# Linear attention into a two-layer MLP on one core: the third batch's x transposed by DMA instead of TensorE, with loads and k preparation of three batches placed elsewhere

## The chip, the core and the metric

The kernel runs on one core of a Trainium2 chip. TensorE (PE) multiplies matrices; VectorE (DVE), ScalarE (ACT) and GpSimd (POOL) do elementwise work; SyncE (SP) issues nearly all DMAs. Each engine runs its own instructions in program order and waits for others by semaphores. The metric is device time in microseconds: the median of three runs before is 295.06 us (294.76 to 298.65).

## The reference

Cosine-weighted linear attention over 8 batches, 8 heads, 576 positions and head width 64, and then a two-layer MLP with a leaky ReLU over the 4608 rows that come out.

```python
def phi(x, c, s):
    r = np.maximum(x, 0.0)
    return np.concatenate([r * c, r * s], axis=-1)   # cos and sin of the position
q_p, k_p = phi(q, cos_w, sin_w), phi(k, cos_w, sin_w)
kv  = np.einsum('bhsf,bhsd->bhfd', k_p, v)
z   = np.sum(k_p, axis=2)
num = np.einsum('bhsf,bhfd->bhsd', q_p, kv)
den = np.einsum('bhsf,bhf->bhs', q_p, z)[..., None] + 1e-06
x = (num / den).transpose(0, 2, 1, 3).reshape(4608, 512)
h = x @ w_in                                         # 512 -> 2048
out = np.maximum(0.01 * h, h) @ w_out                # 2048 -> 512
```

## The kernel before

**Tiles.** Of each batch's 576 positions, 512 are the main part, in four tiles of 128 rows (j = 0 to 3). The 64 left over of all eight batches make a ninth group of 512 rows. So the MLP goes over nine groups g, numbered from 0; the third batch is number 2. All matmuls are in fp16.

**Attention of a batch b.** q, k and v come in as one load of 1 MB each (`load_main`, L86), k and v each with two loads of 64 KB for the left-over rows (`load_kvtail`, L96). `q_prep`, `k_main` and `k_tail` apply phi (L226 on VectorE, L224 on ScalarE). `v_main` and `v_tail` cast v (L232 on ScalarE), with a column of ones for the denominator. `q_transpose_dma` (L334) transposes each q tile by DMA. `kv_all` does 8 matmuls on the left-over rows (L290) and 32 on the main part (L299), and ScalarE copies the result out (L306). `num` does 8 matmuls per tile j (L363), and VectorE divides (L374, L378, L379) and writes x as xs. `num` uses a PSUM pool of one buffer, so the next `num` waits for this divide; `kv_all` uses the same pool.

**x transposed.** The MLP needs x with its 512 columns on the partitions, as xT. For the batches from 3 on this is a DMA transpose per tile (`x_transpose_dma`, L345). For batch 2 it is four TensorE transposes per tile (`x_transpose`, L429) into PSUM and a ScalarE copy (L430). Batches 0 and 1 use TensorE in another form, which the change leaves as it is.

**The MLP.** `f1(g, m)` is four matmuls of 512 columns (L443) for one of 16 column tiles m; after each second one, ScalarE applies the leaky ReLU to the pair (L451). `f2(g, i)` is four matmuls (L466) into an output tile (four calls per tile of 128 rows); after the fourth, VectorE copies the tile out (L234) and SyncE stores it (L480).

**What sets the order.** Past the first two batches the program's order is written by hand. `units` holds f1 and f2 with a position each: 16 positions for each g, in which f2 of g alternates with f1 of g + 1. The table `ahead` says how many f2 calls come before the first f1 of the next batch. All attention work is put in as steps `at(position, function)`, and `weave` emits each step before the first unit whose position is not below its own. A position thus sets the order on every engine and DMA queue; when an instruction really runs depends on its waits. Helpers put whole series at once:

- `load_steps(b, pk, pv, pq)`: k with its two tails at pk, v with its two at pv, q at pq.
- `q_steps(b, start, step, lag)`: q preparation of tile j at start + j step, its DMA transpose lag later.
- `kv_steps(b, start, step, mm, eng_v)`: k tail at start, k pieces every step, v casts on an engine, `kv_all` at mm. The casts begin at start + 3 step, 0.1 apart, for b up to 3, and at start + 1.5 step, 1 apart, for b above 3.
- `out_steps(b, start, step, lag)`: `num` of tile j at start + j step, the DMA transpose of its x lag later.

Each DMA issue on SyncE also waits for the DMA eight before it to land.

Of the kernel before, what the change touches and what calls it, by code (L numbers as in the profile page):

```python
# [9 lines left out]
dt = mybir.dt  # L10
# [3 lines left out]
P = 128  # L14
J = 4
# [3 lines left out]
def kernel(  # L19
# [14 lines left out]
    nc = tc.nc  # L34
# [8 lines left out]
    NKC = DM // P  # L43
# [28 lines left out]
    def psum(where, shape, dtype, name):  # L72
        p = {"h": ps_h, "o": ps_o, "n": ps_n}[where]
        return p.tile(shape, dtype, name=name, tag="ps_" + where)

    st = {}
    ACT, DVE, POOL = nc.scalar, nc.vector, nc.gpsimd
# [85 lines left out]
    def idle(n):  # L163
# [10 lines left out]
    ident = const.tile([P, P], dt.float16, name="ident")  # L174
# [10 lines left out]
        base=0,  # L185
# [3 lines left out]
    for o in range(2):  # L189
# [3 lines left out]
            base=MAIN,  # L193
# [145 lines left out]
    def xT_tile(g, j):  # L339
        if ("xT", g) not in st:  # L340
            st["xT", g] = xtpool.tile([P, NKC, MAIN], dt.float16, name="xT")
        return st["xT", g][:, :, j * P : (j + 1) * P]
# [79 lines left out]
                st["xT", g][:, 2 * hg : 2 * hg + 2, jp * 2 * P : (jp + 1) * 2 * P], ps  # L422
            )

    def x_transpose(g, j, where="o"):
        xs = st["xs", g, j]
        ps = psum(where, [P, NKC, P], dt.float16, "ps_xt")
        for c in range(NKC):
            nc.tensor.transpose(ps[:, c, :], xs[:, 2 * c : 2 * c + 2, :], ident)  # L429
        nc.scalar.copy(xT_tile(g, j), ps)  # L430

    def ffn1(g, m, lo=0, hi=MAIN, chunks=range(NKC), where="h"):
# [117 lines left out]
    ps = psum("h", [P, 2, 512], dt.float32, "ps_numh")  # L552
# [44 lines left out]
    def f1(g, m, where="h"):  # L597
        return lambda: ffn1(g, m, where=where)

    def f2(g, i):  # L600
        return lambda: ffn2(g, i)
# [3 lines left out]
    def at(pos, f, *args):  # L605
        steps.append((pos, lambda: f(*args)))
# [22 lines left out]
    ps = psum("n", [P, 2, DM], dt.float32, "ps_o")  # L629
# [24 lines left out]
    ps = psum("h", [P, 2, MAIN], dt.float16, "ps_x")  # L654
# [22 lines left out]
    for m in range(6, NFT):  # L677
        units.append((8 + m / 2, f1(1, m)))
    for g in range(1, NG):
        ahead = {1: 8, 2: 4}.get(g, 0)  # L680
        order = [f2(g, i) for i in range(ahead)]
        for i in range(16):
            if g + 1 < NG:
                order.append(f1(g + 1, i))
            if ahead + i < 16:
                order.append(f2(g, ahead + i))
        for n, u in enumerate(order):
            units.append((16 * g + 16 * n / len(order), u))
# [3 lines left out]
    def kv_steps(b, start, step, mm, eng_v, n_act=0):  # L692
        at(start - 0.01, kp_tiles, b)
        at(start, k_tail, b, DVE, DVE)
        for i in range(J):
            at(start + (i + 1) * step, k_main, b, i, ACT if i < n_act else DVE, DVE)
        v0, dv = (start + 1.5 * step, 1) if b > 3 else (start + 3 * step, 0.1)
        at(v0, v_main, b, 0, 4, eng_v)
        at(v0 + dv, v_main, b, 4, 8, eng_v)
        at(v0 + 2 * dv, v_tail, b, eng_v)  # L700
        at(mm, kv_all, b)

    def load_steps(b, pk, pv, pq):
        at(pk, load_k, b)
        at(pv, load_v, b)
        at(pq, load_main, "q", q, b)

    def out_steps(b, start, step, lag):
        for j in range(J):
            at(start + j * step, num, b, j)  # L710
            at(start + j * step + lag, x_transpose_dma, b, j)

    def q_steps(b, start, step, lag):
        for j in range(J):
            at(start + j * step, q_prep, b, j)
            at(start + j * step + lag, q_transpose_dma, b, j)

    q_steps(2, 8, 0.4, 0.3)
    kv_steps(2, 9.7, 0.5, 14, DVE, 2)
    for j in range(J):  # L720
        at(14.5 + 1.1 * j, num, 2, j)
        at(15.8 + 1.1 * j, x_transpose, 2, j, "o" if j < 2 else "h")

    load_steps(3, 11, 13, 10)
    q_steps(3, 18, 0.8, 0.8)
    kv_steps(3, 20, 0.7, 24, ACT)
    out_steps(3, 24.5, 1.4, 1)

    load_steps(4, 21.4, 22.5, 21.3)
    kv_steps(4, 28, 1.2, 34, ACT)  # L730
    q_steps(4, 30, 0.8, 0.8)
    out_steps(4, 36.8, 2, 1.6)

    for b in range(5, NG):
        base = 16 * (b - 2)
        if b < B:
            load_steps(b, base - 14.5, base - 13, base - 14.6)
            kv_steps(b, base - 9.5, 1.4, base - 2, ACT)
        else:
            for j in range(J):  # L740
                at(base - 11.5 + 2 * j, load_qtail, j)
        q_steps(b, base - 8, 2, 1)
        out_steps(b, base + 1, 2, 1.6)
# [32 lines left out]
```

## Time and profile before

| what | value |
|---|---|
| median of three runs | 295.06 us |
| the profiled execution | 295.4 us, span 293.6 us, granted TensorE clock 0.999 |
| f1 matmuls, L443 | 592, 142.8 us busy |
| f2 matmuls, L466 | 560, 139.5 us busy |
| x transposes of batch 2, L429 | 16, and 4 ScalarE copies (L430) of 0.58 us |
| DMA transposes: q (L334), x (L345) | 28 and 24, median 3.3 and 3.7 us from issue to landing |
| k, v and q loads of 1 MB | median 9.8, 9.0 and 6.9 us to landing |
| DMA moved | 56.93 MB, mean 194 GB/s |

A row of a timeline or chain is the start in us from the beginning of the span, the length in us, then engine, line, operation and count. Where a wait stands in brackets, it is the idle time before the row and what ended it. In a timeline a matmul group's length includes its way through the array, so groups overlap; in the chain of waits each piece is cut where the next begins, and four matmuls of 512 columns take 0.86 us. The profiled execution's time is its span and 1.8 us around it.

### The profile page before, as it was taken

The page shows a single profiled execution, that of the slowest core. Times are in us where ns is not written, and L with a number is a line of the kernel's source. Part 1 is how long each engine was busy: PE and PEld are TensorE (multiplying, and loading weights), DVE is VectorE, ACT ScalarE, POOL GpSimd, SP SyncE. Part 2 cuts the span into 40 slices and gives each one's busy share as a digit, 9 for nine tenths or more (in the row PEclk, how much of TensorE's full clock was granted, in tenths as well). Part 3 has the DMA queues.
Part 4 walks back from the last instruction along what each step waited for, and adds up shares of the span by engine and source line. Part 5 has one row for each costly group of instructions (what it writes and reads, how often), then busy time and mean ns, then how long its engine had stood idle before and what let it go on. Part 6 is the DMA issues. An engine that isn't in the chain of part 4 may idle for free.

```text
span 293.6 us, 4865 instructions
## 1 busy us (share of the span) xinstructions
PE 286.6 (98%) x1958; PEld 152.6 (52%) x1958; DVE 128.7 (44%) x328; ACT 118.3 (40%) x148; POOL 12.6 (4%) x24
## 2 busy tenths in 40 slices
PE   8899999999999998999999999999999999999995
PEld 3585466555555554555545554555444444444444
DVE  6841687936836714923562346233333311000011
ACT  6856266753544631642453226322222232222200
POOL 2264000000000000000000000000000000000000
PEclk9999999999999999999999999999999999999999
DMA  7999999999999999989664998716671211011133
GB/s 230 346 387 407 321 362 335 313 193 334 200 285 320 180 258 343 163 173 332 170 148 84 279 259 180 111 54 143 136 169 56 71 54 38 36 45 59 42 70 73
DMA packets 88933, 56.93 MB, mean 194 GB/s; under 512 B 56912, under 2 KB 81744, under 8 KB 88528
## 3 DMA queue, kind: packets, MB, share of 16 engines
q1 hardware_dynamic: 88832, 56.57, 74.3%
q8 instruction: 15, 0.25, 0.4%
q10 hardware_dynamic: 80, 0.07, 0.1%
q14 instruction: 6, 0.05, 0.0%
HBM read 36.70 MB, written 9.44 MB: 157 GB/s over the span
## 4 chain that ended last, share of the span: by engine, by line
PE 88%; DMA 6%; SPq 3%; DVE 1%; ACT 1%; issue 0%; DVEq 0%
PE ps_h L443 40%; PE ps_o L466 39%; DMA ktl<-in_k_dram 3%; PE ps_num L363 2%; PE ps_kv L299 2%; DMA vst<-in_v_dram 2%; SPq L96 1%; SPq L86 1%; DMA out_dram<-osb 1%; PE ps_xth L417 1%; PE ps_qt L353 1%; PE ps_numh L399 1%; PE ps_kv L290 0%; PE ps_idle L166 0%; PE ps_kvh L274 0%
## 5 line engine op out<-in xcount | busy, mean ns | idle before, releaser
L443 PE MATMUL ps_h<-xT,w 128*128 128x512 f16 (+1 forms) x592 | 142.8, 373 | 0.1
L466 PE MATMUL ps_o<-w,g 128*128 128x512 f16 x560 | 139.5, 379 | 0.0
L451 ACT ACTIVATE g<-ps_h 128x1024 f16<-128x1024 f32 x72 | 73.2, 1023 | 125.2 <-PE ps_h L443 125.2
L443 PEld LDWEIGHTS <-w 128*128 128x128 f16 x592 | 64.4, 114 | 52.3 <-issue 0.2
L466 PEld LDWEIGHTS <-g 128*128 128x128 f16 x560 | 54.2, 98 | 61.4
L234 DVE COPY osb<-ps_o 128x512 f32<-128x512 f32 x31 | 21.4, 691 | 79.3 <-PE ps_o L466 78.5
L374 DVE TENSOR_SCALAR den<-ps_num 128x8 f32<-128x8 f32 x28 | 4.6, 165 | 51.0 <-PE ps_num L363 51.0
L379 DVE TENSOR_TENSOR xs<-ps_num,rden 128x512 f16<-128x512 f32 x28 | 19.4, 691 | 1.0
L226 DVE TENSOR_SCALAR kpm<-kst,sin_t 128x512 f16<-128x512 f32 (+1 forms) x40 | 16.6, 430 | 1.3 <-DMA kst<-in_k_dram 1.3
L226 DVE TENSOR_SCALAR qp<-qst,cos_t 128x512 f16<-128x512 f32 (+1 forms) x34 | 15.5, 456 | 2.7 <-DMA qst<-in_q_dram 2.7
L226 DVE TENSOR_SCALAR qp<-qst,sin_t 128x512 f16<-128x512 f32 (+1 forms) x34 | 15.5, 456 | 0.0
L232 ACT CAST vmain<-vst 128x1024 f16<-128x1024 f32 (+1 forms) x14 | 12.8, 919 | 6.0 <-DMA vst<-in_v_dram 5.9
L363 PEld LDWEIGHTS <-qpT 128*128 128x128 f16 (+1 forms) x256 | 10.6, 101 | 8.4 <-issue 3.1
L226 DVE TENSOR_SCALAR kpm<-kst,cos_t 128x512 f16<-128x512 f32 (+1 forms) x29 | 13.2, 454 | 0.4 <-DMA kst<-in_k_dram 0.3
L363 PE MATMUL ps_num<-kv,qpT 128*128 128x66 f16 (+1 forms) x256 | 11.8, 194 | 0.9 <-DVE xs L379 0.9
L166 PE MATMUL ps_idle<-blank 128*128 128x512 f16 x30 | 10.0, 483 | 1.2 <-DVE blank L161 1.2
L234 DVE CAST w<-w2st 128x1024 f16<-128x1024 f32 (+1 forms) x6 | 5.1, 868 | 11.5 <-DMA w2st<-in_moe_w_out_dram 11.4
L232 ACT COPY qpT<-ps_qt 128x1024 f16<-128x1024 f16 x7 | 7.0, 1012 | 6.0 <-PE ps_qt L353 6.0
L234 POOL CAST w<-w1st 128x1024 f16<-128x1024 f32 (+1 forms) x9 | 8.5, 946 | 3.4 <-DMA w1st<-in_moe_w_in_dram 3.3
L378 DVE RECIPROCAL rden<-den 128x8 f32<-128x8 f32 x36 | 7.3, 203 | 1.2
L299 PE MATMUL ps_kv<-vmain,kpm 128*128 128x66 f16 x192 | 7.2, 194 | 0.0
L306 ACT CAST kv<-ps_kv 128x528 f16<-128x528 f32 x6 | 3.6, 599 | 7.5 <-PE ps_kv L299 7.5
(62 smaller groups left out, 102.6 us busy)
## 6 DMA issues: line engine op xcount, KB each, us to landing
out_dram<-osb SPq DMA_DIRECT2D x32, 256.0 KB, 2.9
qst<-in_q_dram SPq DMA_DIRECT2D x7, 1024.0 KB, 6.9
kst<-in_k_dram SPq DMA_DIRECT2D x6, 1024.0 KB, 9.8
vst<-in_v_dram SPq DMA_DIRECT2D x6, 1024.0 KB, 9.0
w1st<-in_moe_w_in_dram SPq DMA_DIRECT2D x7, 512.0 KB, 10.3
w2st<-in_moe_w_out_dram SPq DMA_DIRECT2D x3, 1024.0 KB, 12.9
kst<-in_k_dram SPq DMA_DIRECT2D x4, 512.0 KB, 7.2
vst<-in_v_dram SPq DMA_DIRECT2D x4, 512.0 KB, 8.1
```

The costliest lines, as they stand in the source:

```text
L166: nc.tensor.matmul(ps, lhsT=blank[:, 0:P], rhs=blank)
L226: eng.tensor_scalar(out=o, in0=i, scalar1=0.0, scalar2=col, op0=ALU.max, op1=ALU.mult)
L232: nc.scalar.copy(o, i)
L234: eng.tensor_copy(o, i)
L299: nc.tensor.matmul(ps[:, h % 2, h // 2], lhsT=kpm[:, h, j, :], rhs=vmain[b % 2][:, h, j, :], start=False, stop=(h >= H - 2 and j == J - 1),)
L363: nc.tensor.matmul(ps[lo:hi, h // 4, (h % 4) * NE : (h % 4 + 1) * NE], lhsT=qpT[:, h, lo:hi], rhs=kv[b][:, h, :],)
L374: nc.vector.tensor_scalar_add(den.rearrange("p (a b) -> p a b", a=2), ps[:, :, D : 4 * NE : NE], 1e-6)
L378: nc.vector.reciprocal(rden, den)
L379: nc.vector.tensor_tensor(out=xs, in0=ps[:, :, 0 : 4 * NE].rearrange("p a (b e) -> p a b e", e=NE)[:, :, :, 0:D], in1=rden.rearrange("p (a ...
L443: nc.tensor.matmul(ps[:, m % 2, lo:hi], lhsT=w1[m // 4, c][0][:, w1[m // 4, c][1], m % 4 : 512 : 4], rhs=xT[:, c, lo:hi], start=(c == 0 an ...
L451: nc.scalar.activation(st["g", g][:, m - 1 : m + 1, :], ps, AF.Lrelu)
L466: nc.tensor.matmul(st["ps_o", g, tt], lhsT=st["g", g][:, m, tt * P : (tt + 1) * P], rhs=w2[:, m, :], start=(m == 0), stop=(m == NFT - 1),)
```

## The change

- Batch 2's x is transposed by four DMA transposes instead of sixteen TensorE transposes and four ScalarE copies; its `num` steps stand 0.9 apart instead of 1.1 and begin at 14.4 instead of 14.5. `x_transpose` goes.
- Twelve f2 calls of batch 1, instead of eight, stand ahead of the first f1 of batch 2.
- Batch 3's k and v loads move from 11 and 13 to 16.2 and 18, so that on SyncE they come between the x transposes of batch 2: two of these, k and its tails, one, an output, one, v and its tails. Its q load stays at 10. Its q, k, v preparation, `kv_all` and x move back by 0.5 to 1.
- Batch 4's loads move from 21.3 to 22.5 to 24 to 25.1, its preparation and `kv_all` (34 to 36.5) back by 1.5 to 2.5.
- Batch 5's loads come 2 positions later. For batches 5, 6 and 7, the k preparation starts 2 positions later with steps of 1.2 instead of 1.4, and `kv_all` 0.5 later.

Between the second f1 of batch 2 and `kv_all` of batch 3 there are now f2, f1, f2; before there were f2, f1, f2, f1, f2. The v casts of batch 3 stand on ScalarE directly behind the leaky ReLU of that second f1, as before.

```diff
@@ -421,13 +421,6 @@
             nc.scalar.copy(
                 st["xT", g][:, 2 * hg : 2 * hg + 2, jp * 2 * P : (jp + 1) * 2 * P], ps
             )
-
-    def x_transpose(g, j, where="o"):
-        xs = st["xs", g, j]
-        ps = psum(where, [P, NKC, P], dt.float16, "ps_xt")
-        for c in range(NKC):
-            nc.tensor.transpose(ps[:, c, :], xs[:, 2 * c : 2 * c + 2, :], ident)
-        nc.scalar.copy(xT_tile(g, j), ps)
 
 
 
@@ -677,7 +670,7 @@
     for m in range(6, NFT):
         units.append((8 + m / 2, f1(1, m)))
     for g in range(1, NG):
-        ahead = {1: 8, 2: 4}.get(g, 0)
+        ahead = {1: 12, 2: 4}.get(g, 0)
         order = [f2(g, i) for i in range(ahead)]
         for i in range(16):
             if g + 1 < NG:
@@ -717,25 +710,24 @@
 
     q_steps(2, 8, 0.4, 0.3)
     kv_steps(2, 9.7, 0.5, 14, DVE, 2)
-    for j in range(J):
-        at(14.5 + 1.1 * j, num, 2, j)
-        at(15.8 + 1.1 * j, x_transpose, 2, j, "o" if j < 2 else "h")
-
-    load_steps(3, 11, 13, 10)
-    q_steps(3, 18, 0.8, 0.8)
-    kv_steps(3, 20, 0.7, 24, ACT)
-    out_steps(3, 24.5, 1.4, 1)
-
-    load_steps(4, 21.4, 22.5, 21.3)
-    kv_steps(4, 28, 1.2, 34, ACT)
-    q_steps(4, 30, 0.8, 0.8)
-    out_steps(4, 36.8, 2, 1.6)
+    out_steps(2, 14.4, 0.9, 0.8)
+
+    load_steps(3, 16.2, 18, 10)
+    q_steps(3, 18.5, 0.8, 0.8)
+    kv_steps(3, 21, 0.7, 25, ACT)
+    out_steps(3, 25.5, 1.4, 1)
+
+    load_steps(4, 24.1, 25.1, 24)
+    kv_steps(4, 30, 1.2, 36.5, ACT)
+    q_steps(4, 31.5, 0.8, 0.8)
+    out_steps(4, 38, 1.8, 1.6)
 
     for b in range(5, NG):
         base = 16 * (b - 2)
         if b < B:
-            load_steps(b, base - 14.5, base - 13, base - 14.6)
-            kv_steps(b, base - 9.5, 1.4, base - 2, ACT)
+            late = 2 if b == 5 else 0
+            load_steps(b, base - 14.5 + late, base - 13 + late, base - 14.6 + late)
+            kv_steps(b, base - 7.5, 1.2, base - 1.5, ACT)
         else:
             for j in range(J):
                 at(base - 11.5 + 2 * j, load_qtail, j)
```

## The prediction

> **What bounds the kernel now.** I read the page first: shares of the span, then the chain that ended last.
>
> ```profile
> PE 286.6 (98%) x1958; PEld 152.6 (52%) x1958; DVE 128.7 (44%) x328; ACT 118.3 (40%) x148; POOL 12.6 (4%) x24
> ...
> PE 88%; DMA 6%; SPq 3%; DVE 1%; ACT 1%; issue 0%; DVEq 0%
> ```
>
> TensorE is busy 98% of 293.6 us and carries 88% of the chain; the others have slack. So I count two things: work taken off TensorE, and places where it waits. The list of waits, cut to TensorE, has only 0.9 us (for xs, L379) after the start-up. Next the chain in time around the third batch's num and x transposes, and around that wait (start, us, what).
>
> ```profile
> 66.29 0.26 PE ps_num L363 x8
> 66.54 0.22 PE ps_xt L429 x4
> 66.76 1.73 PE ps_o L466 x8
> ```
>
> ```profile
> 105.85 8.51 DMA ktl<-in_k_dram
> ...
> 114.46 0.62 DVE kpt L226 x2
> 115.08 0.09 DVE den L374
> ...
> 116.26 0.42 PE ps_num L363 x8
> 116.67 0.87 PE ps_h L443 x4
> ```
>
> Four transposes cost the chain 0.22 us, four 512-column matmuls 0.86 (call that a unit), a num 0.26. At 114 a k-tail load is late, the VectorE queue stands behind it with a divide in it, and TensorE waits for the divide. Then the ScalarE timeline before kv_all of the fourth batch, and SyncE's around two sets of loads (start, us, engine, line, operation).
>
> ```profile
> 77.54 1.02 ACT L451 ACTIVATE g<-ps_h 128x1024 f16<-128x1024 f32 x1 [2.93 <-PE ps_h L443]
> 78.46 1.98 ACT L232 CAST vmain<-vst 128x1024 f16<-128x1024 f32 x2
> 80.34 0.83 ACT L232 CAST vtail<-vtl 64x256 f16<-64x256 f32 x2
> ```
>
> ```profile
> 62.58 0.80 SPq L86 DMA_DIRECT2D kst<-in_k_dram  x1
> 63.42 4.39 SPq L96 DMA_DIRECT2D ktl<-in_k_dram  x2
> 67.86 0.61 SPq L86 DMA_DIRECT2D vst<-in_v_dram  x1
> ...
> 134.93 0.59 SPq L86 DMA_DIRECT2D vst<-in_v_dram  x1
> 135.62 2.66 SPq L96 DMA_DIRECT2D vtl<-in_v_dram  x2
> ```
>
> The casts end at 81.17, and kv_all starts at 81.76 in the chain: 0.6 us to spare. The v load was issued at 67.86, and a tail pair holds SyncE for 2.66 to 4.39 us. Below, (g,m) is batch index g and column tile m, from 0; f1 is L443, f2 is L466.
>
> **1. Transposes removed.** Four groups of four on TensorE at 0.22 us: -0.88 us. Their ScalarE copies (L430, 0.58 each) go too, from an engine with slack: 0. The four DMA transposes added need no TensorE time.
>
> At this place the Trainium skill speaks against the change: "VectorE: DVE Perf Modes", rules for kernel authors, says to use TensorE for a 128x128 transpose where a PSUM destination will do. Its section on the three transpose paths gives 390 ns by TensorE and 1309 ns by DMA; by the first figure 16 transposes would free 6.2 us (an estimate from that page) and the time would be near 289. The chain's row has 0.055 us each, and I take the row.
>
> **2. Is xT there in time?** Twelve units of f2 instead of eight now stand ahead of f1(2,0): 74.85 + 4 x 0.863 - 0.88 = 77.42. The last divide of this batch ends at 70.8 (num at 69.4, plus 1.42 as in the rows of 63.28 to 64.86). On SyncE the order is two xT, k(3), its tail pair, xT, an output, xT, v(3), its tail pair, then qpT. The second xT is out by 68.3 (xs at 66.85). kst 0.6 and the tail pair 2.66 (the row at 135.62, which like this one has no load directly ahead) give 71.7; xT 1.25, output 0.4, xT 1.25: the last xT is issued at 73.5. Rows of xT behind a set of loads land 3.0 to 4.6 us after issue when issued as second or third (138.97, 140.96, 173.2, 174.6), 6.5 at worst: 76.5 to 78.1, worst 80.0. Wait: 0, ends 0 and 2.6.
>
> **3. The new wait at kv_all(3).** Before, five units lie between the end of f1(2,1) (77.44) and kv_all; now it stands at 25 and only three do, 2.59 us, since the units between have changed. ScalarE must in that time do g of f1(2,0..1) and all v casts, which the program puts behind it: 81.17 - 77.44 = 3.73 us in the rows above, plus about 0.1 to be seen. So TensorE waits 3.73 + 0.1 - 2.59 = 1.25 us even if v has landed. In times: kv_all due at 82.60, possible at 83.85. Behind the waiting matmul stand all of f1(2,3..) and the nums, so the whole of it lengthens the path: +1.25.
>
> **4. v landing.** vst is issued behind the last xT, at 74.8, instead of 67.86. Six 1 MB v loads land 6.9 to 9.7 us after issue: 81.7 to 84.5. ScalarE could cast from 81.15, so it is 0.6 to 3.4 us late; the 6.9 row (134.93) is nearest, because the q load went out 12 us earlier and few bytes are ahead. +0.7, ends 0 and +3.4. A wait in step 2 is absorbed here, since it moves the due time also. VectorE has q, the k tail and eight k halves (0.4 us each) done by about 82.5 (ktl landing near 77.5), ahead of ScalarE. qpT(3,0) goes out at 78.1, and rows behind loads land 6.9 later at worst: 85.0, before its num at about 86.8.
>
> **5. The wait at 114 goes.** Without it f1 would have followed f2 and num at 114.52 + 0.86 + 0.26 = 115.64, where the chain has 116.67: 1.03 us. Loads and k preparation of batch 5 both move by 2, so the distance is the same; what changes is the order on VectorE: the k tail came between num(4,0) and num(4,1), and now stands behind the divide of num(4,1). Counted from f1(3,0): kst goes out near +4.7 (behind an output, two qpT and q), the tail lands 10.1 later as in the row at 104.34, +14.8; num(4,2) comes at +15.7 and only its divide stands behind the tail. num(4,3), at +19.4, would wait if the tail's preparation ended after +18.2; it ends at +15.5. So -1.03, ends -1.03 and 0.
>
> **6. Moves at nothing.** Loads of batch 4 go out at about 84 (they wait for v(3) to land) instead of 82.2, for k preparation that moves from 28 to 30: covered by the six units. xT(3) is then issued from 92 to 97, lands by 100.7 (3.7, the row at 97.0), and f1(3,0) is due at 102; if that cover is gone, up to 2 us. Later batches: the k tail comes 2 later, kv_all 0.5 later, with 2.4 units behind the last k piece for two 0.48 us operations. The last batches' work and the tail of the kernel are untouched.
>
> **Sum.** -0.88 - 1.03 + 1.25 + 0.7 = +0.04 on the profiled execution's 295.4 us (span 293.6 and 1.8 around it). It ran 0.34 over the median 295.06, so in medians: **295.1 us**.
>
> **Rivals.** (a) *The gain stands.* If v and the casts make kv_all in time, only -1.91 is left: 293.2. For it: before, the same casts had 0.6 us to spare, and ScalarE is 40% busy. Against: the count of three units, which needs no transfer to be late. With the structural 1.25 alone and v on time: 294.4.
> (b) *SyncE runs late, so v does* (slower). Place: kv_all(3). If the tail pair takes 4.39 us as at 63.42, each xT 2.2 (the 94.72 row), the output 0.55 and vst 1.1, vst goes out at 78.3 and lands 9.7 later, the casts are done at 90.8, and the wait is 8.3: 295.06 - 1.91 + 8.3 = 301.5. It makes the kernel slower than before as soon as v lands after 81.6, and by over 2% from a wait of 7.8 us. For it: every row of SyncE directly behind 2 MB of loads. Against: here only 1 MB went out some six us earlier. A halfway case (+3.4 at step 4) gives 297.8.
> A gap this long has a second price: the first 14 matmuls on zeros take 5.6 us, 0.40 each, against 0.216 for the same ones at 9.24, so a cold restart could add 14 x 0.184 = 2.6, making 304. The Trainium skill, "TensorE: Matmul & The Clock Gate", part 1, puts the return to half rate at an idle window of about 3.4 us. By that rule only (b) would pay it; the trace's longest gap after start-up, 0.9 us, is followed by a granted clock of 1.00.
> (c) *The wait at 114 only moves.* The same lateness of ktl hits num(4,3): the 1.03 comes back, 296.1. For it: load and use move together. Against: 2.7 us of margin in step 5.
>
> **Chances.** Forecast, 294.3 to 296.6: 0.60. (a) below 294.3: 0.16. (c) about 296.1, within the same band, 0.06. (b) above 296.6: 0.18, of which 0.06 passes 2%. Two per cent is 5.9 us, about what a measurement can tell from no change. All of TensorE's waits and transposes together are below that, so faster by over 2% has 0.02 (out of a), slower 0.06, the rest 0.92. The range takes in (a) at 293.2 and the halfway case of (b): 293.2 to 297.9.
>
> **What would show it.** No ps_xt; the row "PE ps_num <- DVE xs" gone near 114; a new TensorE wait of 1 to 3 us at L290 for vtail from ScalarE near 83, with "vmain <- vst" ahead of it on ScalarE; f1(2,0) starting at 77.4 with no wait for xT. It is wrong if there is no wait at L290, if TensorE waits for xT, or if a wait of over a us stands in batches 3 to 8.

## The result and the profile after

The changed kernel takes 298.2 us (median of 22 runs, 297.12 to 300.59); the kernel before took 295.35 beside it (22 runs). The ratio is 1.0103, with a 95% interval of 1.0081 to 1.0126: about 3 us slower, clear of noise, and just outside the range that was predicted. The ratios here and below are of executions that lie within 1.5% of the fastest of their kernel; the few that ran longer are left out of them.

The profiled execution's time is 297.58, its span 295.8. First the shares of the page, after:

```profile
PE 285.7 (97%) x1942; PEld 151.8 (51%) x1942; DVE 128.5 (43%) x328; ACT 116.5 (39%) x144; POOL 12.6 (4%) x24
...
PE 86%; DMA 6%; DVE 2%; ACT 2%; SPq 2%; issue 1%; ACTq 0%; DVEq 0%
```

Sixteen instructions and 0.9 us of work have left TensorE, yet the span is longer. TensorE works less and waits more. The list of waits (who waited, for whom: us in all, times, longest), TensorE's own rows:

```profile
PE ps_h L436 <- DMA xT<-xs: 2.8, 2, 1.8
...
PE ps_kv L290 <- ACT vtail L232: 1.0, 2, 0.8
```

Neither row was there before, and the row for num and xs is gone. The same places in the chain of waits (start, us, what):

```profile
71.91 5.99 DMA xT<-xs
...
77.94 1.02 PE ps_h L436 x4
...
80.78 0.09 ACT g L444
...
81.71 1.98 ACT vmain L232 x2
...
84.47 0.28 PE ps_kv L290 x7
...
100.08 4.00 DMA xT<-xs
...
104.21 1.03 PE ps_h L436 x4
```

Read it from the bottom. f1(3,0) starts at 104.21, when the last x transpose of batch 3 lands; TensorE had no work from 102.45 on. kv_all(3) starts when ScalarE has done g, vmain and vtail. f1(2,0) starts at 77.94 for a transpose issued at 71.91 that took 6 us. SyncE's timeline shows what stands around those two transposes:

```profile
73.18 0.57 SPq L86 DMA_DIRECT2D vst<-in_v_dram  x1
73.80 1.41 SPq L96 DMA_DIRECT2D vtl<-in_v_dram  x2
75.33 3.96 SPq L334 DMA_TRANSPOSE qpT<-qp  x1
...
86.08 0.53 SPq L86 DMA_DIRECT2D qst<-in_q_dram  x1
...
95.17 6.12 SPq L345 DMA_TRANSPOSE xT<-xs  x4
```

The loads of batch 4 begin at 86.08, and the four x transposes of batch 3 come out in one block from 95.17, though three of their tiles were ready by 94. Before, the loads began at 82.23, and the x transposes went out in two pairs, the first of them four us sooner:

```profile
82.23 0.53 SPq L86 DMA_DIRECT2D qst<-in_q_dram  x1
...
91.41 2.62 SPq L345 DMA_TRANSPOSE xT<-xs  x2
...
94.72 3.48 SPq L345 DMA_TRANSPOSE xT<-xs  x2
```

Executions start unevenly: kv_all(2) begins anywhere from 60.6 to 62.1 us, and TensorE's waits differ in the first 20 us, which the change does not touch. So I compare traces from the first matmul of kv_all(2) to the first of the last output tile (L495 before, L488 after), both from TensorE's timeline. Before: 286.51 - 61.16 = 225.35. After: 288.41 - 60.63 = 227.78. By parts, from the chain:

| term | forecast | measured |
|---|---|---|
| 16 transposes off TensorE | -0.88 | -0.88 |
| wait at 115 for xs, behind batch 5's k tail | -1.03 | -1.03 |
| kv_all(3) waits for the casts (85.87 less 77.94 + 5.18 + 1.36) | +1.25 | +1.4 |
| more there, because v lands late | +0.7 | 0 |
| f1(2,0) waits for xT (77.94 less 76.88) | 0 | +1.06 |
| f1(3,0) waits for xT (104.21 less 102.45) | 0 | +1.76 |
| sum | +0.04 | +2.3 of the 2.43 seen |

The measured column mixes two ways of counting. If every term is counted by when a matmul starts and when it could have started, f1(2,0) loses 1.22, f1(3,0) 1.93 and kv_all(3) 1.35, of which 0.1 was there before (its last f2 began at 80.73, kv_all at 81.69, 0.96 later instead of 0.86); the wait at 115 was worth 1.07. The sum is then 2.45, which accounts for the whole of the 2.43.

### The profile page after: what moved, and what is told of

It reads as the page before. It is cut to its first block, busy times and chain, and to the rows that moved or that the text cites. A ratio compares the mean times of both kernels' runs of the same rounds, so it can differ in the third digit from the quotient of the medians.

```text
span 295.8 us, 4843 instructions
## 1 busy us (share of the span) xinstructions
PE 285.7 (97%) x1942; PEld 151.8 (51%) x1942; DVE 128.5 (43%) x328; ACT 116.5 (39%) x144; POOL 12.6 (4%) x24
## 4 chain that ended last, share of the span: by engine, by line
PE 86%; DMA 6%; DVE 2%; ACT 2%; SPq 2%; issue 1%; ACTq 0%; DVEq 0%
PE ps_h L436 41%; PE ps_o L459 37%; DMA xT<-xs 3%; PE ps_num L363 3%; PE ps_kv L299 2%; DMA vst<-in_v_dram 2%; ACT vmain L232 1%; SPq L96 1%; DMA out_dram<-osb 1%; DVE qp L226 1%; PE ps_xth L417 1%; PE ps_qt L353 1%; PE ps_numh L399 1%; SPq L86 1%; PE ps_kv L290 0%
## 5 line engine op out<-in xcount | busy, mean ns | idle before, releaser
L234 DVE COPY osb<-ps_o 128x512 f32<-128x512 f32 x31 | 21.4, 691 | 83.4 <-PE ps_o L459 81.7
```

What stands on the lines that cost most here:

```text
L234: eng.tensor_copy(o, i)
```

## The experiments

The theory from this profile: three waits, each with its cause in an order (ScalarE's casts, SyncE's loads ahead of transposes). The rival: the DMA engines themselves are full there, and four more transposes must come back as some wait. All runs beside the kernel before; "stretch" is the span from kv_all(2) to the last output tile.

| run | ratio to before, 95% interval | stretch, us | TensorE waits in it |
|---|---|---|---|
| before | 1 | 225.35 | num 0.9 |
| changed | 1.0103 (1.0081 to 1.0126) | 227.78 | f1(2,0), kv_all(3), f1(3,0) |
| casts_first | 1.0113 (1.0073 to 1.0153) | 227.46 | the same three |
| v4_behind_x | 1.0096 (1.0064 to 1.0129) | 229.54, clock 0.994 | the same three |
| k3_early | 1.0097 (1.0059 to 1.0134) | 226.44 | kv_all(3), f1(3,0) 1.64 |
| ahead8 | 1.0112 (1.0082 to 1.0142) | 228.05 | f1(2,0) 1.67, kv_all(3), f1(3,m) on g |
| all_covered | 1.0091 (1.0071 to 1.0111) | 227.86 | f1(3,0) 0.61, num 1.34, f1 on g 1.53 |
| q4_late | 1.0249 (1.0217 to 1.0281) | 232.74, clock 0.989 | num 4.34, f1(2,0) 0.65, kv_all(3) |
| x2_dma_old_places | 1.0157 (1.0124 to 1.0190) | 230.79, clock 0.987 | f1(2,0) 4.98 |
| x2_on_pe | 1.0026 (1.0006 to 1.0046) | 225.53 | kv_all(3) |
| x2_on_pe_kv3_late | 1.0007 (0.9981 to 1.0032) | 225.17 | f1(3,0) 0.71 |
| late_part_only | 0.9989 (0.9962 to 1.0016) | 224.29 | none |
| late_part_again | 0.9969 (0.9956 to 0.9982) | 224.28 | none |
| four_more_full | 1.0049 (1.0017 to 1.0082) | 225.69 | f2(2,15) on g 1.06 |
| four_more_empty | 0.9982 (0.9955 to 1.0009) | 224.29 | none |

The stretch and the waits are of one profiled execution each, the ratio of all. One execution is a rough measure: up to f1(2,0) the changed kernel, casts_first, v4_behind_x, q4_late and ahead8 are the same program, and their traces show waits of 1.06, 0.64, 2.09, 0.65 and 1.67 us there. Where the mean clock is below 0.995, a long wait was followed by some us at half the granted clock, which lengthens the stretch beyond the wait; the last section shows it.

### One wait at a time

casts_first puts the v casts of batch 3 ahead of g on ScalarE:

```diff
         v0, dv = (start + 1.5 * step, 1) if b > 3 else (start + 3 * step, 0.1)
+        if b == 3:
+            v0, dv = 22.9, 0.01
```

> The changed kernel, with the v casts of batch 3 put ahead of the leaky ReLU of f1(2,0..1) on ScalarE instead of behind it. In the changed kernel kv_all(3) starts 1.33 us later than the six units before it allow (84.45 for 83.12), and ScalarE runs the leaky ReLU first and the casts then. Theory (order on ScalarE): the casts start when v lands, near 80.5, and end near 83.2, so the wait at kv_all(3) falls from 1.33 to about 0.2 us and the span by about 1.1. Rival (v lands late): v lands near 81.7 anyway, the casts keep their time, and nothing is gained. Second rival: all of the gain comes back at the wait of f1(3,0) for xT, since SyncE and the DMA queues don't move; then that wait grows from 1.8 to 2.8 us and the span stays.

The casts began at 81.05, about when v landed (80.9), and the wait at kv_all(3) fell from 1.4 to 0.95. The wait at f1(3,0) grew from 1.76 to 2.31. So less was won than forecast, since v landed barely earlier than ScalarE was free, and what was won, there and at f1(2,0) (0.64 for 1.06), came back in good part one wait later, as the second rival has it. The time is the changed kernel's.

v4_behind_x and q4_late move loads of batch 4 behind transposes of batch 3:

```diff
-    load_steps(4, 24.1, 25.1, 24)
+    load_steps(4, 24.1, 28, 24)          # v4_behind_x
+    load_steps(4, 24.1, 25.1, 31)        # q4_late, with
+    q_steps(4, 34.9, 0.3, 0.1)
+            late = 2.7 if b == 5 else 0
```

> The changed kernel, with the v loads of batch 4 at position 28 instead of 25.1, so that on SyncE they stand behind the first two x transposes of batch 3 instead of ahead of all four. Theory (place on SyncE): in the changed kernel all four x transposes of batch 3 are issued from 95.2 on, behind the whole set of loads, though three of the tiles are ready by 94; with v behind, the first two go out by 93, the last one lands about 2 us earlier, and f1(3,0) no longer waits: -1.5 to -1.8 us, with v(4) still in time for its casts. Rival (the bytes decide): the same bytes go through the same DMA engines before the last transpose is wanted, which lands no earlier: 0. Second rival: v(4) is late and kv_all(4) waits instead: 0 or slower.

> The changed kernel, with 1 MB less on SyncE and the DMA engines ahead of batch 3's x transposes: the q load of batch 4 at 31 instead of 24, behind them, its preparation at 34.9 in steps of 0.3, and batch 5's loads 0.7 later. Theory (bytes ahead of xT(3) on full DMA engines make f1(3,0) wait): k and v of batch 4 are out about 3 us earlier, xT(3) lands 2 to 3 us earlier, and the wait of 1.76 at f1(3,0) goes: -1.5 to -1.8. Rival (SyncE's waits for the landing of earlier DMAs set the time, not the bytes): the loads end only 0.6 us earlier and the wait stays above 1. Second rival: q(4) or the k tail of batch 5 is late and a num waits: 0 or slower.

With v behind the first two, the wait at f1(3,0) was 0.80 instead of 1.76, but this does not show that SyncE's order was to blame. The last x transpose did not land 2 us sooner, as the theory has it: it landed 45.1 us after kv_all(2), in the changed kernel 43.4. TensorE was later still, because f1(2,0) had waited 2.09 and the next two units then ran at half clock, 1.7 us more. The stretch adds up with that: 227.78 + 1.03 - 0.96 + 1.69 = 229.54. The time of all executions did not move. With q behind, the last x transpose landed 40.8 us after kv_all(2), 2.7 sooner, as forecast, and the wait at f1(3,0) went; q and the k tail of batch 5 were late instead. VectorE's timeline of q4_late shows the second rival:

```profile
118.71 0.48 DVE L226 TENSOR_SCALAR qp<-qst,cos_t 128x512 f16<-128x512 f32 x1 [1.82 <-DMA qst<-in_q_dram]
...
123.96 0.35 DVE L226 TENSOR_SCALAR kpt<-ktl,cos_t 128x256 f16<-128x256 f32 x1 [4.37 <-DMA ktl<-in_k_dram]
```

A num stood 4.34 us behind that. Half clock followed here too (granted 0.50 from 126 to 132) and cost 2.8 us more, and the ratio is 1.0249.

k3_early puts batch 3's k load ahead of all four transposes of batch 2; ahead8 wants xT of batch 3 later; all_covered does both and moves kv_all(3):

```diff
-    load_steps(3, 16.2, 18, 10)
+    load_steps(3, 11, 18, 10)                   # k3_early, all_covered
-        ahead = {1: 12, 2: 4}.get(g, 0)
+        ahead = {1: 12, 2: 8}.get(g, 0)         # ahead8, all_covered
-    kv_steps(3, 21, 0.7, 25, ACT)
-    out_steps(3, 25.5, 1.4, 1)
+    kv_steps(3, 21, 0.7, 26, ACT)               # all_covered
+    out_steps(3, 26.5, 1.2, 1)
```

> The changed kernel, with batch 3's k load back at 11, so that on SyncE k and its tails go out right behind q(3), ahead of all four x transposes of batch 2; v stays behind them. Theory (the wait of f1(2,0) comes from the k load issued ahead of the last two transposes): k has landed by 72, the last xT lands near 76 instead of 77.9, and that wait falls from 1.06 to 0; v goes out no earlier than before. The wait at kv_all(3) stays at 1.4 and that at f1(3,0) grows by up to 1.1, since the loads of batch 4 do not move: between 0 and -1.1 in the whole. Rival (the DMA engines are full from 62 us on, and the order of the same bytes doesn't matter): xT lands no earlier, and the time is the changed kernel's.

> The changed kernel with eight f2 calls of batch 2, instead of four, ahead of f1(3,0): no work more or less, but xT of batch 3 is wanted 3.45 us later. Theory: the wait of 1.76 us at f1(3,0) goes and nothing takes its place; the waits at f1(2,0) (1.06) and kv_all(3) (1.4) stay; from kv_all(2) to the last output tile 226.0 us instead of 227.8. Rival (full DMA engines make something else late): another TensorE wait of over 1 us turns up behind it, as the k tail of batch 5, and the time stays.

> The changed kernel with all three waits covered: batch 3's k load at 11, ahead of the x transposes; kv_all(3) at 26 and its num steps from 26.5 in steps of 1.2; eight f2 calls ahead of f1(3,0). Theory: no TensorE wait over 0.3 us is left after the start-up, the transposes' 0.88 and the wait at 115 (1.03) are won, and from kv_all(2) to the last output tile it takes 223.4 us against 225.35 in the kernel before: ratio 0.993 to 0.995. Rival (the added transposes on full DMA engines always come back as some wait): a new wait, at f1(4,0) or a num of batch 4 or 5, and the time is that of before or above.

In k3_early the wait at f1(2,0) is gone and the stretch is 1.3 us shorter, as its theory said; the timed ratio is too coarse to show it. In ahead8 it is the wait at f1(3,0) that is gone, but behind it TensorE waits for g, because ScalarE stands before a cast of batch 5's v. all_covered fell as a theory: with every known wait covered, the list of waits has two new ones and a rest at f1(3,0).

```profile
PE ps_h L436 <- ACT g L444: 1.5, 2, 0.8
PE ps_num L363 <- DVE xs L379: 1.3, 1, 1.3
...
PE ps_h L436 <- DMA xT<-xs: 0.6, 1, 0.6
```

VectorE's timeline leads the middle one back to the k tail of batch 5 (3.54 us of waiting for ktl before it), and the chain leads the first to v tails. Three orders are repaired, and the whole is as slow as before the repair. That points away from any single order, but doesn't prove it, since the repair moved steps of its own.

### The swap against the new places

x2_on_pe keeps all new places and puts the transposes back on TensorE; x2_dma_old_places is the kernel before with the swap and nothing else.

```diff
-    out_steps(2, 14.4, 0.9, 0.8)
+    for j in range(J):                          # x2_on_pe
+        at(14.4 + 0.9 * j, num, 2, j)
+        at(15.7 + 0.9 * j, x_transpose, 2, j, "o" if j < 2 else "h")
```

```diff
-        ahead = {1: 8, 2: 4}.get(g, 0)          # x2_dma_old_places, from before
+        ahead = {1: 12, 2: 4}.get(g, 0)
-    for j in range(J):
-        at(14.5 + 1.1 * j, num, 2, j)
-        at(15.8 + 1.1 * j, x_transpose, 2, j, "o" if j < 2 else "h")
+    out_steps(2, 14.5, 1.1, 1.3)
```

> The changed kernel, with batch 2's x transposed on TensorE again (16 transposes and 4 ScalarE copies), all loads and steps at the changed places. Theory: +0.88 us of TensorE work, -1.06 for the wait of f1(2,0) for xT, and SyncE runs 2.5 to 5 us earlier behind it, so that the loads of batch 4 go out before 86 and the wait at f1(3,0) falls from 1.76 to under 0.7; together -1.0 to -2.0. The wait at kv_all(3) stays, 1.2 to 1.4. Rival (the places alone make it slow): the waits at kv_all(3) and f1(3,0) stay as they are, and the sum is -0.2, no difference that a run can tell.

> The kernel before with only the swap: batch 2's x by DMA transposes at its old places, and twelve f2 calls ahead instead of eight; every load and every other step as before. Theory (four transposes are added to DMA engines that are full from 62 to 102 us in the profile before): xT of batch 2 stands behind the whole of batch 3's loads, is issued from 73 on, the last lands near 81, and f1(2,0), due at 77.4, waits 3 to 4 us; the loads of batch 4 go out 3 to 5 us later than the 82.2 of before, and f1(3,0) waits for xT too. Together with -0.88 and the wait at 115 (which stays): 297.5 to 301. Rival (the new places of the loads make it slow, not the swap): at most 1 us slower than before.

Back on TensorE, both waits for xT are gone, the one at kv_all(3) stays, and the ratio falls from 1.0103 to 1.0026. The stretches differ by 2.25 us, and these terms give it: 0.88 for the transposes against 1.22 and 1.93 for the two waits. The swap alone is the worse half: 1.0157, since f1(2,0) waits 4.98 for transposes that stand behind 3 MB. Half clock after this gap costs another 2.3 us (granted 0.50 from 82 to 86). Against the expectation neither f1(3,0) nor the num at 115 waits in that run. So the new places seem a help to the swap (1.0103 against 1.0157), and not enough. How busy the DMA engines are is seen in the table of stretches (the last two columns are DMA share and GB/s; the share counts packets that overlap, so it passes 1, and a share near 1 does not prove that no engine is free). Before, then the changed kernel, then x2_on_pe:

```profile
62.00:70.00 8.00, 8.00 (x81) 4.78 (x78) 3.19 (x9) 3.99 (x6) 0.00 (x0) 1.00 1.02 261
70.00:78.00 8.00, 8.00 (x52) 4.13 (x50) 6.30 (x16) 1.63 (x3) 0.00 (x0) 1.00 1.22 258
```

```profile
62.00:70.00 8.00, 8.00 (x67) 4.33 (x64) 3.96 (x12) 2.65 (x3) 0.00 (x0) 1.00 1.10 208
70.00:78.00 8.00, 6.95 (x33) 3.12 (x32) 6.29 (x16) 0.00 (x0) 0.00 (x0) 1.00 1.23 239
```

```profile
62.00:70.00 8.00, 8.00 (x98) 5.08 (x99) 3.19 (x9) 4.37 (x6) 0.00 (x0) 1.00 1.00 290
70.00:78.00 8.00, 8.00 (x51) 4.02 (x50) 5.62 (x14) 1.53 (x3) 0.00 (x0) 1.00 0.61 169
```

Before, the share is 1.02 and 1.22. In the changed kernel the engines move fewer bytes, 208 and 239 GB/s, at as high a share: transposes take their time without moving much. Only with the new places and without the transposes is there clear slack, 0.61.

x2_on_pe_kv3_late moves kv_all(3) from 25 to 26 there, with the two lines shown for all_covered.

> The changed places with batch 2's x on TensorE, as in the run x2_on_pe, and kv_all(3) at 26 instead of 25 with its num steps from 26.5: two more units of f1 stand between f1(2,1) and kv_all. Theory (the wait at kv_all(3) is the three units left to ScalarE for 3.7 us of work): that wait, 1.4 us, goes; no TensorE wait over 0.5 us is left after the start-up, and the kernel is 1.1 us faster than before, 293.9 to 294.5. Rival (v lands late): the wait only moves with its place and stays above 0.7. Second rival: f1(3,0) waits for xT instead, since num(3,3) comes later.

The wait at kv_all(3) is gone, so it was the three units that the change left to ScalarE. But 0.71 comes up at f1(3,0), which is reached sooner, and the gain isn't measurable.

### Four transposes that nobody waits for

late_part_only is the kernel before with only the last part of the change, batches 5 to 7; late_part_again repeats it. four_more_full and four_more_empty add to it four transposes without a reader. They leave nothing of the computation out.

```diff
+    def spare_transpose(j):
+        spare = kv[4 + j].rearrange("p h e -> p (h e)")[:, 0:DM]     # kv[j] in four_more_empty
+        nc.sync.dma_start_transpose(
+            out=spare.rearrange("p (c x) -> p c x", c=NKC), in_=w2[:, j, :]
+        )
+        at(15.8 + 1.1 * j, spare_transpose, j)                       # 104.8 in four_more_empty
```

> The kernel before, with only the last part of the change: batch 5's loads 2 positions later, and for batches 5, 6 and 7 the k preparation 2 later in steps of 1.2 and kv_all 0.5 later. Theory: the k tail of batch 5 then stands behind the divide of num(4,1) on VectorE, the wait of 0.9 us at 115 goes, and the kernel is 0.8 to 1.1 us faster than before, with no new wait. Rival: the load moves with its use, the tail is as late as it was, and another num waits: 0.

> The kernel of late_part_only once more, beside the other two on one chip, since its first interval did not tell a gain of 0.3% from none. Theory: 0.996 to 0.998 of before, and about 0.3% above all_covered, the 0.88 us of TensorE transposes that it keeps. Rival: no difference from before, though its trace has no wait at 115.

> The kernel of late_part_only (which has no TensorE wait after the start-up) with four more DMA transposes of 128 by 512 fp16, from the MLP's second weights into space that is not yet in use, at 15.8 to 19.1, behind the loads of batch 3; nothing reads their results and TensorE's work is the same. Theory (DMA engines full from 62 us on; four transposes take them 4 to 5 us): the loads of batch 4 go out 3 us or more later than in late_part_only, counted from kv_all(2), and a TensorE wait of 0.5 to 3 us turns up behind, at f1(3,0) for xT or at a num of batch 4; ratio to the kernel before 0.999 to 1.006. Rival (only the new places of the changed kernel's steps make the waits): no new wait, ratio 0.996 to 0.998 as without them.

> The same four transposes without a reader, at 104.8 to 108.1, where the profile shows the DMA engines busy a tenth of the time. Theory: no wait, ratio 0.996 to 0.998 as in late_part_only. Rival (a DMA transpose costs wherever it is put, by SyncE's queue or the memory): slower by what the other run shows.

The late part alone takes the wait at 115 away: the stretch is 1.06 us shorter in both executions. The first interval holds 1; the second, 0.9956 to 0.9982, does not. It is the fastest kernel here, at 294.19 us.

The four spare transposes show that added transposes cost time by themselves, whatever the places of the other steps. At 15.8 they cost 1.4 us of the stretch, although no engine waits for them. The loads of batch 4 begin 23.1 us after kv_all(2) instead of 20.4, 2.7 later. So batch 4's v lands late on ScalarE, as its timeline in four_more_full shows:

```profile
98.91 1.05 ACT L232 CAST vmain<-vst 128x1024 f16<-128x1024 f32 x1 [2.59 <-DMA vst<-in_v_dram]
...
101.72 1.03 ACT L451 ACTIVATE g<-ps_h 128x1024 f16<-128x1024 f32 x1
```

That g ends 1.06 us after f2(2,15) could have begun; the wait was forecast for f1(3,0) or a num. At 104.8, where the page gives the DMA engines a tenth, the same four land 2.4 to 3.4 us after issue and cost nothing. The intervals of the two runs, 1.0017 to 1.0082 and 0.9955 to 1.0009, don't meet.

Whether it is the DMA engines' time or SyncE's that runs out, these runs don't tell. SyncE's timeline in four_more_full just ahead of the loads, and the table of stretches there:

```profile
78.92 1.26 SPq L720 DMA_TRANSPOSE kv<-w  x1
80.28 0.52 SPq L480 DMA_DIRECT2D out_dram<-osb  x1
80.91 4.03 SPq L334 DMA_TRANSPOSE qpT<-qp  x3
85.03 0.53 SPq L86 DMA_DIRECT2D qst<-in_q_dram  x1
```

```profile
78.00:82.00 4.00, 4.00 (x20) 1.96 (x19) 3.67 (x10) 3.65 (x6) 0.00 (x0) 1.00 0.87 158
82.00:86.00 4.00, 4.00 (x61) 2.53 (x60) 1.59 (x4) 1.58 (x2) 0.00 (x0) 1.00 1.02 197
```

SyncE issues one DMA right behind the other. It takes 1.3 us for each transpose, hardly more than the 1.2 that the spare ones take in four_more_empty, and the DMA share is 0.87 and 1.02. So here the loads wait for SyncE's issuing. In q4_late it is rather the engines: with 1 MB less ahead of them, 0.5 us of SyncE's time, batch 4's k and v loads were all out 31.1 us after kv_all(2) instead of 33.8, and only 0.4 of that is an earlier start. A transpose takes time of both, and in this stretch neither has much to spare.

### The loads on a queue of their own

after_pool_loads is the changed kernel with the loads from batch 3 on issued by GpSimd; all_covered_pool is all_covered with the same edit.

```diff
-        nc.sync.dma_start(
+        (POOL if b > 2 else nc.sync).dma_start(     # load_main, and so in load_kvtail
```

> The changed kernel with all q, k and v loads from batch 3 on issued from GpSimd's queue, which has no other work by then, instead of SyncE's; transposes and outputs stay on SyncE. Theory A (SyncE's one queue makes the transposes late): the waits for xT at f1(2,0) and f1(3,0) go, 2.8 us together, only the 1.4 at kv_all(3) may stay, and the ratio is near 1.000. Theory B (the DMA engines have no time left from 62 to 120 us): the sum of the TensorE waits stays at 3 us or more, since the loads now compete with the transposes packet by packet, and the ratio stays at 1.01 or above.

> The kernel of all_covered with the loads from batch 3 on issued from GpSimd's queue. Theory A: no TensorE wait over 0.3 us after the start-up, 223.4 us from kv_all(2) to the last output tile, ratio 0.993 to 0.996. Theory B: waits of 2 us or more in sum remain, at transposes or at the k and v of batches 4 and 5, and the ratio is 1.005 or above.

Both are far slower: 330.7 us at best and 332.9 at best, beside 295.26. That is on theory B's side, and by far more than its 1.01. The loads no longer stand in SyncE's order and run ahead as far as their buffers let them: in after_pool_loads batch 3's v load goes out at 51.0 instead of 73.2. What stays on SyncE loses against them: the four qpT of batch 2 held it for 16.2 us instead of 7.8. It shows that a second queue doesn't help in this form, and that SyncE's order was also what kept the loads from running ahead. Since the loads run at another time, it doesn't tell SyncE's time and the engines' apart either. The Trainium skill says in "DMA: Bandwidth & Descriptors", section "Issuing engines are not separate DMA queues", that DMAs of all issuing engines run on the same 16 DMA engines and interleave; the 16.2 us agree with it.

## Why the prediction was wrong

**Right.** The transposes' 0.88 (step 1). The wait at 115 (step 5), which late_part_only shows alone. The wait at kv_all(3) by the count of three units (step 3): 1.25 more than before by start times, as forecast, and gone in x2_on_pe_kv3_late. The Trainium skill's 390 ns for a transpose ("VectorE: DVE Perf Modes", The three transpose paths) would have freed 6.2 us by the estimate in step 1; the trace's 0.055 each, 0.88 in all, stood.

**Wrong, the step that failed: step 2, "Wait: 0".** The last xT was issued at 71.91, even sooner than the forecast 73.5. I gave it 3.0 to 4.6 us to land and it took 5.99. These numbers came from rows at 139 to 175 us. The rows of the crowded stretch itself, 91.41 to 94.72 in the kernel before, took 6.5, 6.4 and 5.5 us, and I had put 6.5 down as the worst case only. In k3_early, where k goes out ahead of all four, the last xT landed 2.8 us after issue and f1(2,0) did not wait. The wait was 1.06 here, within the bound of 2.6 that the step itself gave.

**Wrong, step 4.** v landed 7.6 us after issue, at 80.8, not at 81.7 or later, because it was issued 1.6 us sooner (0.5 of that is this execution's earlier kv_all(2)). The 0.7 did not arise, so step 2's wait was not absorbed there as the step said, and counted in full.

**Wrong, step 6, "Moves at nothing".** It had the last x transpose of batch 3 issued by 97 and landed by 100.7, and named up to 2 us if that cover were gone. It was issued at 100.08, landed at 104.07, and cost 1.76, the largest of the terms that I had at nothing. I had followed SyncE's queue row by row up to batch 3, but not carried the four added transposes on through it. four_more_full shows what they do to it by themselves: the next loads begin 2.7 us later. In the changed kernel these begin 25.5 us after kv_all(2), where before it was 21.1. In x2_on_pe, with the new places and without the added transposes, it is 22.8, so 1.7 of the 4.4 belong to the places and 2.7 to the transposes.

**Rivals.** (b), SyncE late, was the right mechanism in the wrong place: at xT of two batches, not at v in kv_all(3). Its halfway time, 297.8, is near the 298.2 measured, but by luck: it is made of another wait. Its second price, a cold restart, was no part of the changed kernel's profiled execution, but it came in v4_behind_x, q4_late and x2_dma_old_places. (a) and (c) did not occur. The "about 2%" that a measurement was said to tell was too coarse: here the interval is 0.45% wide.

**The missing term** was the time that the added transposes take from the DMA queue. Each wait was weighed alone, and the transposes were priced on TensorE and at their landing, but not as work for SyncE (1.2 us each or more, 5 us in all) and for DMA engines whose share is 0.94 or more in every stretch of 4 us from 62 to 102 us before. That the transposes cause the waits is shown by x2_on_pe and the spare ones; which of the two resources sets the 2.7 us stays open.

The Trainium skill's rule in "VectorE: DVE Perf Modes", to prefer TensorE for a 128x128 transpose with a PSUM destination, held here: x2_on_pe at 1.0026 against 1.0103. four_more_empty suggests where it need not hold: there four transposes by DMA cost nothing.

## What to carry to other kernels

Before work goes from a busy engine to DMA, look at the DMA share and at the issuing queue's timeline in the stretch in which it will run, and carry the added time through the queue to every later load, not only to its own reader. If one covered wait is followed by the next, look for a full resource instead of a wrong order. To price an operation on a shared resource, add it without a reader, once where the resource is full and once where it is idle. And read a wait from more than one execution before a theory rests on it.

## What the runs showed of the hardware

A transpose of 128 by 512 fp16, 128 KB, holds SyncE for 1.2 us or more, and in four_more_empty, with nearly idle engines, lands after 2.4 us. Four in a row took 6.12 us at 95.17 in the changed kernel. One transpose is thus dear for its size: 128 KB in 1.2 us are 109 GB/s, while the loads ran at 354 GB/s between 88 and 90 us before, 3 us for 1 MB.

In after_pool_loads TensorE stood still for 12.55 us at once, and the granted clock fell. Its table of stretches (the third column from the right is the clock):

```profile
62.00:70.00 8.00, 0.46 (x3) 0.09 (x1) 0.00 (x0) 1.02 (x1) 1.25 (x2) 0.80 1.04 325
70.00:78.00 8.00, 2.37 (x39) 2.00 (x39) 3.00 (x6) 0.00 (x0) 3.16 (x4) 0.50 1.17 287
```

0.50 is the half rate that the Trainium skill, "TensorE: Matmul & The Clock Gate", part 1, gives for a TensorE that has been idle for a window. The waits of the changed kernel, 1.8 us at most, leave the clock at 1.00.

A gap well below the 3.4 us that the prediction cites from the Trainium skill can be enough; where the two differ, the trace decides. In v4_behind_x TensorE waited 2.09 us, and its timeline and the table of stretches show half clock soon after (four matmuls in 1.91 us instead of 1.03):

```profile
79.45 1.06 PE L436 MATMUL ps_h<-xT,w 128*128 128x512 f16 x4 [2.09 <-DMA xT<-xs]
80.31 1.91 PE L459 MATMUL ps_o<-w,g 128*128 128x512 f16 x4
```

```profile
81.00:82.00 1.00, 1.00 (x3) 0.30 (x2) 0.31 (x1) 0.00 (x0) 0.00 (x0) 0.50 1.15 316
```

In casts_first a gap of 2.31 us left the clock at 1.00, so its length alone does not decide. What else does, these runs don't show.
